# One block kernel: attention's transfers issued later, turned token groups split in alternation, half of the first norms on ScalarE, one store moved

## The chip, the cores and the metric

The kernel runs on one core of one Trainium2 chip. The metric is the device time of one execution in microseconds (us): the median of three runs, and one more execution under the hardware profiler.

## What is computed

The input is 2048 tokens of width 576. They are normalized, and the normalized tokens go two ways: through attention with 32 heads of width 18 and a sliding window of 256, and through a gated feed-forward block with a 2048 x 2048 matrix that mixes tokens. The two results are multiplied and added to the input.

```
xn = layernorm(x)
q, k, v = split(xn @ wqkv)                       # 32 heads of 18
o = softmax(mask(q k^T / sqrt(18), 0 <= i - j < 256)) v
s = o @ wo
z = gelu(xn @ w_in);  z1, z2 = halves of 2304
g = w_sp @ layernorm(z2) + b_sp                  # over tokens
out = x + s * silu((z1 * g) @ w_out)
```

## The kernel before, in words

All products run in float32 halves: an operand is split into a high part (rounded by ScalarE, `split`, L112) and a low part (the difference, by VectorE, L113), and three products of halves are summed. TensorE is the engine with most of the work. The other engines' instructions, and the queue of SyncE (SP), which issues every DMA, stand in an order that the Python code writes out by hand; each queue is worked off strictly in that order, so an instruction that waits holds up what stands behind it.

The stages, in order of time:

- **Tokens in, q and k (0 to 156 us).** Tokens come in four chunks of 512 (`load_x`). VectorE takes their means and variances (`stats_of`, `scales_of`), and a norm writes them to `xpair` (on VectorE for chunk 0, `norm_dve` L316; on ScalarE for the others, `norm_act` L323). TensorE turns them in groups (`turn_group`, L333): group one has planes 0 to 3, group two planes 4 to 7, each in one PSUM tile `tpt`, and group three plane 8, in a tile that one of the first two has to give back. The function that `turn_group` returns splits a group plane by plane: high by ScalarE, low by VectorE. The planes lie in `b0` to `b5`. Then the weights of q and k, fetched into three buffers `wraw` and split by ScalarE (`wqh`) and GpSimd (`wql`), are multiplied with the planes: first narrow products of 256 columns (`first_steps` L418, `narrow` L369), then wide ones of 512 (`qk_wide`, L203). Each result is split into `qkhl` and stored in `st_d` by four DMAs (`keep_chunk` L359, `keep` L352).
- **v, z2 (156 to 440 us).** The same planes times other weights.
- **Attention (440 to 950 us).** There are 16 units (4 heads by 1024 tokens). For a unit, rows q and k of its heads are loaded from `st_d` into slots `att` (L539): 16 DMAs at the start of each unit, called a burst below, of which the first 8 are for the second pair of heads of the next unit and the last 8 for the first pair of the one after. A burst stands behind four small DMAs `att<-mhl` (L619) that bring in row maxima. Scores for the maxima (`sp`, L589), scores for the exponentials (`tps`, L713, exponentials `pt` on ScalarE L717, masks on GpSimd L725 and L728) and the product with v (`ops`, L741) are put in order by a planner: it keeps a clock, gives each instruction a fixed cost, and takes a loaded pair as there 5500 ns after its last load is issued (`LOAD_NS`). Where nothing is ready it fills in products of z1 (L660), whose weights `z1raw` (L629) ScalarE splits (`z1wh`, L675) and whose results `z1o` are stored in `z_d` (L562 calls the store).
- **The end of a unit** (`finish`): denominators `den` are loaded from `ou` (L803), VectorE inverts them (L776), they are stored in `r_d` (L778) and fetched back spread over partitions by four DMAs `rp` (L783, 128 KB each), GpSimd multiplies (`divide`, L787, four pieces), and four DMAs store `o_d` (L792). The times of these steps after the end of the unit, in the planner's ns, are the constants `INVERT_AT`, `FETCH_AT` (after the store of `r_d`) and `DIVIDE_AT` (four divides, four stores).
- **Output of attention (950 to 1010 us)**, with `ohl` (L1123) split from `o_d`; **mixing over tokens (to about 1715 us)** and **last product with silu (to 1939 us)**.

Of the kernel before, what the change touches and what calls it, by code (L numbers as in the profile page):

```python
# [16 lines left out]
P = 128  # L17
# [27 lines left out]
MAX_NS = 5000  # L45
INVERT_AT = 7500
FETCH_AT = 3500
DIVIDE_AT = (18000, 19500, 21000, 22500, 23500, 24000, 24500, 25000)
WARM = 54
# [7 lines left out]
def f32(ap):  # L57
    return ap.bitcast(F32)
# [3 lines left out]
def kernel(  # L62
# [169 lines left out]
    with ExitStack() as early:  # L232
# [17 lines left out]
        with ExitStack() as ph:  # L250
# [75 lines left out]
            def turn_group(c, ks):  # L326

                t = tp.tile([P, 2, 512], F32, name="tpt")
                for n, k in enumerate(ks):
                    for i in range(2):  # L330
                        for h, r in enumerate(ROWS):
                            c0 = (2 * n + i) * 64
                            pe.transpose(t[:, h, c0:c0 + 64], xpair[c][i][r, k].rearrange("p a b -> p (a b)"),  # L333
                                         ident[r, r])

                def form():
                    for n, k in enumerate(ks):
                        src = t[:, :, n * P:(n + 1) * P].rearrange("p h (i d) -> p i h d", i=2)
                        cs = slice(c * 256, (c + 1) * 256)
                        hi, lo = (plane(m, cs).rearrange("p (i h d) -> p i h d", i=2, h=2) for m in (k, 9 + k))  # L340
                        split(hi, lo, src)

                return form

# [53 lines left out]
            for tiles in ((0, 1), (2, 3)):  # L398
                stats_of(0, tiles)
                scales_of(0, tiles)  # L400
            for i in range(4):
                done = norm_dve(0, i)
# [17 lines left out]

            forms[0]()
            forms[1]()
            first_steps(WL_LAST[0:8])
            turn_group(0, [8])()
            first_steps(WL_LAST[9:17])
            first_steps([24, 25])
# [22 lines left out]
            load_x(3)  # L449
            forms[0]()  # L450
            forms[1]()
            scales_of(2, range(4))
            banks = narrow(4, 0)
            turn_group(1, [8])()
            fetch(6, w_qk[6])
            keep_narrow(4, 0, banks)
            for j in range(5):
                banks = narrow(j, 1)
                if j < 2:
                    fetch(7 + j, w_qk[7 + j])  # L460
                if j == 3:
                    forms = [turn_group(2, range(0, 4)), turn_group(2, range(4, 8))]
                keep_narrow(j, 1, banks)
                done = None
                if j < 2:
                    norm_act(2, (2 * j, 2 * j + 1))
                if j == 0:
                    stats_of(3, range(4))
                if j == 1:
                    done = scales_of(3, range(4))  # L470
                if j == 3:
                    forms[0]()
                    forms[1]()
                if j == 4:
                    turn_group(2, [8])()
                    norm_act(3, range(4))
                if j < 4:
                    wq_high(5 + j)
                    low = wq_low(5 + j)
                    if done:  # L480
                        behind(low, done)
            for j in range(5, 9):
                if j < 8:
                    fetch_v(0, j - 5)
                for n in qk_wide(j, 0):
                    if j == 6 and n in (3, 9, 18):
                        turn_group(3, (range(0, 4), range(4, 8), [8])[(3, 9, 18).index(n)])()
                if j < 8:
                    split_v(wv, 0, j - 5)
            tokens.close()  # L490
# [18 lines left out]
        with ExitStack() as ph:  # L509
# [138 lines left out]
            def z1_rows(r):  # L648

                for f in range(FH // P):  # L650
# [6 lines left out]
                    for b in range(2):  # L657
                        ps = fillp.tile([P, 512], F32, name=("ma", "mb")[r])
                        for n, (w, x_) in enumerate(moving_x(wh, wl, slice(b * 512, (b + 1) * 512), r)):
# [3 lines left out]
                            if n == STEPS - 1:  # L663
                                zo = zw.tile([P, 512], F32, name="z1o", bufs=3)
                                act.activation(zo, ps, AF.Copy)  # L665
                                bank_free[r] = use("act", 480, 120) + 100
                                after(bank_free[r] - clock + 100,
                                      partial(sp.dma_start, z1_tokens[f * P:(f + 1) * P, b, :, r],
                                              zo.rearrange("p (a q) -> p a q", a=2)))
# [99 lines left out]
            def finish(u, ou):  # L769
# [5 lines left out]
                def invert():  # L775
                    dve.reciprocal(den, den)  # L776
# [207 lines left out]
            with ExitStack() as heads:  # L984
# [64 lines left out]
                while score_queue[0] or score_queue[1] or todo or filling:  # L1049
# [498 lines left out]
```

## Time and profile before

| what | value |
|---|---|
| median of the runs | 1942.09 us (1939.25 to 1943.32, three runs) |
| the profiled execution: its own time, its span | 1941.25 us, 1939.5 us |
| TensorE busy, share of the span | 1876.8 us, 97% |
| VectorE, ScalarE, GpSimd busy | 1038.2, 914.3, 397.6 us |
| granted TensorE clock, mean | 0.984 |
| DMA: moved, mean rate | 389.85 MB, 201 GB/s |

The span runs from the first to the last instruction. In the rows of the timeline, the columns are start in us, duration in us, engine, line, operation, output and inputs, shape, count, and in brackets the idle time of the engine before the row and what ended it. SPq rows are DMA issues. In rows of waits the columns are the total in us, the number of waits and the longest. A row of windows gives, after the stretch and its length, the busy time of TensorE, of its weight loads, of VectorE, ScalarE and GpSimd with the number of instructions, then the granted clock, the DMA share and GB/s.

### The profile page before, as it was taken

What the parts mean: (1) busy time and instruction counts of PE and PEld (TensorE: products, weight loads), DVE (VectorE), ACT (ScalarE), POOL (GpSimd) and SP (SyncE); (2) the same over time, 40 slices, a digit from 0 to 9 for tenths busy, and PEclk for the clock granted to TensorE, in tenths of its full rate; (3) what the DMA queues carried; (4) which work ended last, traced back from release to release, by engine and by line L of the source; (5) the groups of instructions that cost most, each with busy time, mean ns of one, the idle gap of its engine ahead of it and who ended that gap; (6) DMA issues with size and microseconds to landing.
All of it is one profiled execution on the core that took longest, in us unless ns stands there. A gap on an engine that the chain in (4) does not pass through costs nothing.

```text
span 1939.5 us, 38538 instructions
## 1 busy us (share of the span) xinstructions
PE 1876.8 (97%) x14552; PEld 1627.8 (84%) x14552; DVE 1038.2 (54%) x2275; ACT 914.3 (47%) x1758; POOL 397.6 (20%) x486
## 2 busy tenths in 40 slices
PE   8999999999999998999899999999999999999999
PEld 7899999997777776766698878888888888899998
DVE  5411333456567655654227787747786667563222
ACT  4523322324656654666548575555454534442111
POOL 3322333434455444545300000000000000000000
PEclk7999999999999998999899999999999999999999
DMA  7786688885656655564577777766676555875441
GB/s 228 181 222 181 215 280 277 285 279 150 166 162 177 184 147 151 151 177 113 181 248 261 234 243 237 248 221 217 199 251 234 184 176 180 272 231 155 143 141 58
DMA packets 234314, 389.85 MB, mean 201 GB/s; under 512 B 51984, under 2 KB 145680, under 8 KB 234000
## 3 DMA queue, kind: packets, MB, share of 16 engines
q1 hardware_dynamic: 234128, 387.39, 64.6%
q8 instruction: 114, 1.87, 0.4%
q14 instruction: 72, 0.59, 0.1%
HBM read 274.74 MB, written 111.78 MB: 199 GB/s over the span
## 4 chain that ended last, share of the span: by engine, by line
PE 78%; DMA 9%; DVE 5%; SPq 3%; issue 2%; ACT 2%; POOL 1%; POOLq 0%; DVEq 0%; ACTq 0%
PE acc L1378 31%; PE po L1471 12%; PE mb L203 10%; PE ma L660 5%; PE ma L203 4%; PE mb L660 4%; PE ops L741 4%; DMA att<-st_d 3%; PE tps L713 2%; PE sp L589 2%; PE wops L1137 2%; DMA z1raw<-in_w_z_dram 1%; SPq L352 1%; DMA den<-ou 1%; DMA st_d<-qkhl 1%
## 5 line engine op out<-in xcount | busy, mean ns | idle before, releaser
L1378 PE MATMUL acc<-spl,zh 128*128 128x512 f32 x1008 | 392.6, 390 | 1.9 <-DVE spl L113 1.7
L1378 PE MATMUL acc<-sph,zh 128*128 128x512 f32 x1008 | 392.2, 389 | 0.0
L1378 PE MATMUL acc<-sph,zl 128*128 128x512 f32 x1008 | 392.1, 389 | 0.0
L593 DVE CUSTOM_DVE_ANT_0 junk<-sp,band 128x384 bf16<-128x384 f32 (+1 forms) x512 | 275.8, 539 | 177.5 <-PE sp L589 78.3
L717 ACT ACTIVATE pt<-tps 128x384 f32<-128x384 f32 (+2 forms) x576 | 230.3, 439 | 151.3 <-PE tps L713 102.5
L660 PE MATMUL mb<-b,z1wh 64*128 64x512 f32 x648 | 228.2, 406 | 0.4 <-ACT z1o L665 0.3
L660 PE MATMUL ma<-b,z1wh 64*128 64x512 f32 x648 | 227.0, 406 | 0.5 <-ACT zt L935 0.4
L1378 PEld LDWEIGHTS acc<-spl,zh 128*128 128x128 f32 x1008 | 189.2, 188 | 42.9 <-DVE spl L113 3.5
L113 DVE TENSOR_TENSOR spl<-spr,sph 128x1024 fp32r<-128x1024 f32 x168 | 205.6, 1224 | 32.8 <-ACT sph L112 32.2
L1378 PEld LDWEIGHTS acc<-sph,zh 128*128 128x128 f32 x1008 | 189.2, 188 | 39.6
L1378 PEld LDWEIGHTS acc<-sph,zl 128*128 128x128 f32 x1008 | 189.2, 188 | 38.6
L112 ACT ACTIVATE zh<-b 128x384 fp32r<-128x384 f32 x168 | 87.4, 520 | 230.3 <-PE acc L1378 230.3
L713 PE MATMUL tps<-att 56*128 56x384 f32 (+1 forms) x576 | 180.3, 354 | 10.4 <-ACT pt L717 7.7
L589 PE MATMUL sp<-att 54*128 54x384 f32 (+1 forms) x512 | 162.8, 359 | 19.5 <-DMA att<-st_d 14.6
L112 ACT ACTIVATE sph<-spr 128x1024 fp32r<-128x1024 f32 x168 | 175.8, 1047 | 2.1 <-DMA spr<-in_w_sp_dram 1.3
L113 DVE TENSOR_TENSOR zl<-b,zh 128x384 fp32r<-128x384 f32 x168 | 93.4, 556 | 147.0 <-ACT zh L112 146.9
L1471 PE MATMUL po<-b,yh 128*128 128x288 f32 x840 | 147.2, 295 | 0.5 <-ACT gs L1458 0.5
L713 PEld LDWEIGHTS tps<-att 56*128 56x128 f32 x576 | 100.7, 189 | 41.9 <-ACT pt L717 16.6
L660 PE MATMUL ma<-b,z1wl 64*128 64x512 f32 x324 | 130.3, 402 | 0.0
L660 PE MATMUL mb<-b,z1wl 64*128 64x512 f32 x324 | 130.1, 402 | 0.0
L589 PEld LDWEIGHTS sp<-att 54*128 54x128 f32 x512 | 89.7, 189 | 45.1 <-issue 22.8
L660 PEld LDWEIGHTS ma<-b,z1wh 64*128 64x128 f32 x648 | 119.9, 190 | 6.6 <-issue 1.8
(232 smaller groups left out, 4228.5 us busy)
## 6 DMA issues: line engine op xcount, KB each, us to landing
spr<-sc_d SPq DMA_DIRECT2D x96, 512.0 KB
spr<-in_w_sp_dram SPq DMA_DIRECT2D x72, 512.0 KB
zr<-z_d SPq DMA_DIRECT2D x144, 192.0 KB
z_d<-zt SPq DMA_DIRECT2D x48, 384.0 KB
z_d<-z1o SPq DMA_DIRECT2D x72, 256.0 KB
z1t<-z_d SPq DMA_DIRECT2D x72, 256.0 KB
y_d<-z1t SPq DMA_DIRECT2D x72, 256.0 KB
a<-in_w_sp_dram SPq DMA_DIRECT2D x64, 256.0 KB
```

The source lines that it names most:

```text
L112: act.activation(hi, src, AF.Copy)
L113: dve.tensor_tensor(lo, src, f32(hi), ALU.subtract)
L203: pe.matmul(banks[h][:, :n], *both[h][i], start=i == 0, stop=i == STEPS - 1)
L589: pe.matmul(ps[:, :w], q_of(u, j)[0:54, i * P:(i + 1) * P], k_of(u, j)[0:54, k0:k0 + w], start=True, stop=True)
L593: dve.tensor_tensor_reduce(out=junk[:, :w], in0=ps[:, :w], in1=band[:, m0:m0 + w], scale=1.0, scalar=-3.0e38, op0=ALU.add, op1=ALU.max, ac ...
L660: pe.matmul(ps, w, x_, start=n == 0, stop=n == STEPS - 1)
L713: pe.matmul(ps[:, :m * P], k_of(u, j)[:, (kb - base) * P:(kb - base + 1) * P], q_of(u, j)[:, (a - lo) * P:(a - lo + m) * P], start=True, s ...
L717: act.activation(pt[:, j, d0:d0 + n * P], ps[:, (qa - a) * P:(qa - a + n) * P], AF.Exp, scale=scale)
L741: pe.matmul(o_ps[c][32 * j:32 * j + 32, (qa - 4 * c) * P:(hi - 4 * c + 1) * P], vgs[u][:, kb - k0, j * VW:j * VW + 32], pt[:, j, (qa - kb) ...
L1137: pe.matmul(po[:, i, :288], lt[:, cs], r[:, i * 288:(i + 1) * 288], start=n == 0, stop=n == len(pl) - 1)
L1378: pe.matmul(acc[j], z[:, ps], w[:, cs], start=s == i == 0 and n in OPENS, stop=s == 7 and i == 2, skip_group_check=True)
L1471: pe.matmul(po[i][:, a, :288], y if ahead else y[:, i * P:(i + 1) * P], w[a], start=f == 0 and m == 0, stop=f == NF - 1 and m == 2)
```

## The change

Five edits:

1. The function returned by `turn_group` is now a list of pieces, and `form(*groups)` splits two groups in alternation: the high halves of plane k of both groups on ScalarE, then both low halves on VectorE. The first products on chunk 0 take the planes in that order (0, 4, 1, 5, ...).
2. Of the four norms of chunk 0, those of tiles 0 and 1 go to ScalarE (`norm_act`).
3. The splits of the first half of v's weights (`split_v(wv, ...)`) come one product later, so behind the splits of chunk 3.
4. In attention the store of `z1o` comes 1200 instead of 100 ns after the planned copy; the load of `den` 1000 instead of 300; inversion, store of `r_d`, fetch of `rp`, the divides and the stores of `o_d` all later.
5. At the end of attention, what the planner has due within 3000 ns is issued ahead of the loads for the output product, the rest behind them.

```
-INVERT_AT = 7500
-FETCH_AT = 3500
-DIVIDE_AT = (18000, 19500, 21000, 22500, 23500, 24000, 24500, 25000)
+KEEP_NS = 1200
+INVERT_AT = 9000
+FETCH_AT = 7500
+DIVIDE_AT = (22500, 24000, 25500, 27000, 31000, 31500, 32000, 32500)
...
+            def form(*groups):
+                for pieces in zip(*groups):
+                    for hi, _, src in pieces:
+                        act.activation(hi, src, AF.Copy)
+                    for hi, lo, src in pieces:
+                        dve.tensor_tensor(lo, src, f32(hi), ALU.subtract)
...
                 scales_of(0, tiles)
-            for i in range(4):
+                if tiles[0] == 0:
+                    norm_act(0, tiles)
+            for i in (2, 3):
                 done = norm_dve(0, i)
...
-            forms[0]()
-            forms[1]()
-            first_steps(WL_LAST[0:8])
-            turn_group(0, [8])()
-            first_steps(WL_LAST[9:17])
+            form(*forms)
+            ready = (0, 4, 1, 5, 2, 6, 3, 7)
+            first_steps([3 * k for k in ready])
+            form(turn_group(0, [8]))
+            first_steps([3 * k + 1 for k in ready])
...
-                if j < 8:
-                    split_v(wv, 0, j - 5)
+                if j > 5:
+                    split_v(wv, 0, j - 6)
...
-                                after(bank_free[r] - clock + 100,
+                                after(bank_free[r] - clock + KEEP_NS,
...
-                    after(t, lambda: sp.dma_start(r_d[u].rearrange("h (a b) -> (h a) b", b=HS // 32), den))
+                    after(t + 1500, lambda: sp.dma_start(r_d[u].rearrange("h (a b) -> (h a) b", b=HS // 32), den))
...
-                    after(busy["act"] - clock + 300, lambda: sp.dma_start(den, ou[DH::32, :]))
+                    after(busy["act"] - clock + 1000, lambda: sp.dma_start(den, ou[DH::32, :]))
...
-                oraws += [wo_load(t) for t in range(1, 3)]
-                while waiting:
-                    clock += 100000
-                    tick()
+                for ns in (3000, 100000):
+                    waiting.sort(key=lambda w: w[0])
+                    while waiting and waiting[0][0] <= clock + ns:
+                        waiting.pop(0)[1]()
+                        waiting.sort(key=lambda w: w[0])
+                    if ns == 3000:
+                        oraws += [wo_load(t) for t in range(1, 3)]
```

**ScalarE, the first chunk, before.** `tpt_248` and `tpt_265` are the PSUM tiles of groups one and two, `tpt_336` that of group three; `st` are statistics.

```order
L116 ACTIVATE st1_205<-st2_204,eps_t_87 128x2 x2
L265 ACTIVATE wqh_242<-wraw_189 128x1152
L265 ACTIVATE wqh_245<-wraw_191 128x1152
L112 ACTIVATE b0_92<-tpt_248 128x256 x3
L112 ACTIVATE b1_93<-tpt_248 128x256
L112 ACTIVATE b1_93<-tpt_265 128x256 x2
L112 ACTIVATE b2_94<-tpt_265 128x256 x2
L112 ACTIVATE b2_94<-tpt_336 128x256
```

The same place in the changed kernel (lines past 333 have other numbers there).

```order
L117 ACTIVATE st1_205<-st2_204,eps_t_87 128x2
L324 ACTIVATE xpair_222<-xr_181,st3_206,st4_207 128x9x64
L324 ACTIVATE xpair_223<-xr_183,st3_206,st4_207 128x9x64
L117 ACTIVATE st1_205<-st2_204,eps_t_87 128x2
L266 ACTIVATE wqh_242<-wraw_189 128x1152
L266 ACTIVATE wqh_245<-wraw_191 128x1152
L349 ACTIVATE b0_92<-tpt_248 128x256
L349 ACTIVATE b1_93<-tpt_265 128x256
L349 ACTIVATE b0_92<-tpt_248 128x256
L349 ACTIVATE b1_93<-tpt_265 128x256
```

Two norms now stand between the two square roots, and the reads go to the two tiles in turn.

**SP, the second burst of attention, before** (the one at 512.38 us in the trace of before): the DMAs from the store of `r_d` to the burst's eighth load.

```order
L778 DMA r_d<-den 128x32
L783 DMA rp<-r_d 32x1024
L562 DMA z_d<-z1o 128x2x256
L783 DMA rp<-r_d 32x1024 x3
L562 DMA z_d<-z1o 128x2x256
L619 DMA att_6848<-mhl 2x8x128 x2
L619 DMA att_2227<-mhl 2x8x128 x2
L539 DMA att_2229<-st_d 36x1024
L539 DMA att_2229<-st_d 18x1024 x2
L539 DMA att_2229<-st_d 36x1024 x2
L539 DMA att_2229<-st_d 18x1024 x2
L539 DMA att_2229<-st_d 36x1024
```

The same place in the changed kernel, from the row maxima to the eighth load.

```order
L627 DMA att_6848<-mhl 2x8x128 x2
L627 DMA att_2227<-mhl 2x8x128 x2
L547 DMA att_2229<-st_d 36x1024
L791 DMA rp<-r_d 32x1024
L547 DMA att_2229<-st_d 18x1024
L791 DMA rp<-r_d 32x1024
L547 DMA att_2229<-st_d 18x1024
L791 DMA rp<-r_d 32x1024
L547 DMA att_2229<-st_d 36x1024
L791 DMA rp<-r_d 32x1024
L547 DMA att_2229<-st_d 36x1024
L547 DMA att_2229<-st_d 18x1024 x2
```

The four fetches of `rp`, which stood ahead of the maxima, now stand among the first loads. The same holds for the next five bursts, through the one at 648.32 us.

**SP, the burst at 716.54 us, before**, from the maxima to the third load.

```order
L619 DMA att_6846<-mhl 2x8x128 x2
L619 DMA att_6848<-mhl 2x8x128 x2
L783 DMA rp<-r_d 32x1024 x4
L562 DMA z_d<-z1o 128x2x256
L792 DMA o_d<-ou 18x1024
L539 DMA att_2228<-st_d 36x1024
L792 DMA o_d<-ou 18x1024
L539 DMA att_2228<-st_d 18x1280
L629 DMA z1raw<-in_w_z_dram 128x1152
L792 DMA o_d<-ou 18x1024
L562 DMA z_d<-z1o 128x2x256
L539 DMA att_2228<-st_d 18x1024
```

The same place in the changed kernel.

```order
L627 DMA att_6846<-mhl 2x8x128 x2
L627 DMA att_6848<-mhl 2x8x128 x2
L786 DMA r_d<-den 128x32
L570 DMA z_d<-z1o 128x2x256
L791 DMA rp<-r_d 32x1024 x4
L547 DMA att_2228<-st_d 36x1024
L637 DMA z1raw<-in_w_z_dram 128x1152
L547 DMA att_2228<-st_d 18x1280
L547 DMA att_2228<-st_d 18x1024
L547 DMA att_2228<-st_d 36x1280
L570 DMA z_d<-z1o 128x2x256
L547 DMA att_2228<-st_d 36x1024
```

The four stores of `o_d` are gone from among the loads (they now stand behind the burst before, with the same unit's divides ahead of them on GpSimd), and `z1raw` has moved up.

More of the change, by code (lines that the diff above doesn't have):

```diff
@@ L334, in turn_group @@
                                          ident[r, r])
[L336 to L343, printed above, removed]
+                pieces = []
+                for n, k in enumerate(ks):
+                    src = t[:, :, n * P:(n + 1) * P].rearrange("p h (i d) -> p i h d", i=2)
+                    cs = slice(c * 256, (c + 1) * 256)
+                    hi, lo = (plane(m, cs).rearrange("p (i h d) -> p i h d", i=2, h=2) for m in (k, 9 + k))
+                    pieces.append((hi, lo, src))
+                return pieces
+            def form(*groups):
[4 more added lines that the diff above has]
+                        dve.tensor_tensor(lo, src, f32(hi), ALU.subtract)
             st_v = st_d.rearrange("n r h (b a g p) -> n r h b a g p", b=2, a=2, g=2)
@@ L449 @@
             load_x(3)
-            forms[0]()
-            forms[1]()
+            form(*forms)
             scales_of(2, range(4))
             banks = narrow(4, 0)
-            turn_group(1, [8])()
+            form(turn_group(1, [8]))
             fetch(6, w_qk[6])
@@ L471 @@
                 if j == 3:
-                    forms[0]()
-                    forms[1]()
+                    form(*forms)
                 if j == 4:
-                    turn_group(2, [8])()
+                    form(turn_group(2, [8]))
                     norm_act(3, range(4))
@@ L486 @@
                     if j == 6 and n in (3, 9, 18):
-                        turn_group(3, (range(0, 4), range(4, 8), [8])[(3, 9, 18).index(n)])()
-                if j < 8:
-                    split_v(wv, 0, j - 5)
+                        form(turn_group(3, (range(0, 4), range(4, 8), [8])[(3, 9, 18).index(n)]))
+                if j > 5:
+                    split_v(wv, 0, j - 6)
             tokens.close()
```

## The prediction

> **What bounds the kernel now.** I read the table of windows first, for four stretches cut at the stages.
>
> ```profile
> 0.00:95.00 95.00, 81.66 (x952) 75.48 (x954) 48.55 (x150) 45.93 (x93) 30.20 (x22) 0.87 0.72 205
> 95.00:440.00 345.00, 343.13 (x3974) 338.30 (x3973) 122.75 (x245) 95.66 (x211) 121.02 (x109) 1.00 0.79 246
> 440.00:960.00 520.00, 479.68 (x4468) 362.10 (x4465) 292.09 (x1047) 307.28 (x745) 242.82 (x355) 0.96 0.58 161
> 960.00:1939.00 979.00, 972.37 (x5167) 851.89 (x5165) 574.80 (x834) 465.44 (x710) 3.53 (x2) 1.00 0.64 206
> ```
>
> The first busy time is TensorE's. It leaves 13.3 us idle up to 95 us, 40.3 us in attention (440 to 960), and 1.9 and 6.6 us elsewhere. TensorE is the bound, the change touches none of its work, and so it can win only from these idle times and from the clock they cost (the column 0.87 and 0.96). The waits of TensorE grouped by what released it follow.
>
> ```profile
> PE sp L589 <- DMA att<-st_d: 14.6, 8, 2.9
> PE tps L713 <- ACT pt L717: 7.7, 4, 4.1
> ```
>
> In attention what ends last is mostly a load `att`: 14.6 us in 8 waits, at most 2.9. One of them in the timeline, and the window of 4 us behind it:
>
> ```profile
> 491.88 0.38 PE L589 MATMUL sp<-att 54*128 54x256 f32 x2 [1.94 <-DMA att<-st_d]
> 492.00:496.00 4.00, 4.00 (x28) 3.92 (x30) 2.09 (x9) 1.78 (x4) 1.23 (x2) 0.64 0.82 196
> ```
>
> The granted clock is 0.64 in that window, so (1 - 0.64) x 4 = 1.4 us are lost beyond the wait of 1.94, in all some 3.4. I take 1.5 us for such a dip, and that not every wait has one is a source of error. The Trainium skill, "TensorE: Matmul & The Clock Gate", section "Why this matters for your kernels", says that only idle gaps of over about 3 us between bursts of matmuls bring the half clock back. The trace disagrees (1.94 us was enough); by that rule the dips behind the shorter gaps below would drop out on both sides, and the sum would come out about 1.4 us later.
>
> **The front (0 to 95 us).**
>
> ```profile
> 10.88 3.21 DVE L316 TENSOR_SCALAR xpair<-xr,st,st 128x576 f32<-128x576 f32 x4
> 15.19 0.38 ACT L112 ACTIVATE b<-tpt 128x256 fp32r<-128x256 f32 x1 [3.38 <-PE tpt L333]
> ...
> 20.77 0.38 ACT L112 ACTIVATE b<-tpt 128x256 fp32r<-128x256 f32 x1 [0.49 <-DVE b L113]
> 22.68 0.42 DVE L113 TENSOR_TENSOR b<-tpt,b 128x256 fp32r<-128x256 f32 x1 [1.07 <-ACT b L112]
> 29.02 0.38 PE L369 MATMUL ma<-b,wqh 64*128 64x256 f32 x1 [0.74 <-DVE qkhl L113]
> 30.25 3.15 ACT L323 ACTIVATE xpair<-xr,st,st 128x576 f32<-128x576 f32 x4
> ```
>
> Four norms on VectorE take 3.21 us, 0.80 each; on ScalarE 3.15, as long. Two of them go to an engine that stood idle (3.38 us before its first split), so the chain of VectorE is 2 x 0.80 = 1.6 us shorter. The high parts of planes 0 and 7 are 20.77 - 15.19 = 5.58 us apart, 0.80 per plane: each 0.38 on ScalarE waits for the 0.42 on VectorE before it, because both read the same PSUM tile. In alternation the pace is VectorE's 0.42, and 7 x (0.80 - 0.42) = 2.7, less about 0.5 for the turns of the second group, which are now needed sooner: 2.2 us. Together 3.8. TensorE waits at 29.02 for VectorE's `qkhl`, at the end of the same chain, so I take it in full; at the least the 0.74 of that wait.
>
> ```profile
> 41.98 0.34 PE L333 MATMUL tpt<-ident,xpair 64*128 64x64 f32 x4 [1.99 <-DVE b L113]
> ...
> 79.10 0.34 PE L333 MATMUL tpt<-ident,xpair 64*128 64x64 f32 x4 [3.61 <-DVE b L113]
> 80.00:84.00 4.00, 4.00 (x24) 3.59 (x22) 2.38 (x6) 2.72 (x6) 0.00 (x0) 0.57 0.36 82
> 90.60 17.75 SPq L352 DMA_DIRECT2D st_d<-qkhl  x24
> ```
>
> On chunk 1 the third group of turns waits 1.99 us for the splits of a tile; faster splits take away 1.5 of it (bounds 0.4, what one plane saves, and 4, the wait with a clock dip). On chunk 3 the same turn waits 3.61 us, since the splits stand on ScalarE behind `wvh`, whose weights come late by DMA; `split_v` one product later removes that: 3.6, plus (1 - 0.57) x 4 = 1.7 of clock, less 0.3 for the splits themselves: 5.0. The later `wvh` now stands in front of nothing that is due within a product. Front: 3.8 + 1.5 + 5.0 = 10.3. Behind it lies a stretch in which SP's queue is the limit: 24 stores in a row take 17.75 us, 0.74 each. When TensorE comes there sooner it can end up waiting for a `qkhl` that has not been stored. I give 1.3 back (all of it but 1: rival C): 9.0.
>
> **Attention, the losses.**
>
> ```profile
> 512.38 5.65 SPq L539 DMA_DIRECT2D att<-st_d  x12
> 520.74 0.62 PE L589 MATMUL sp<-att 54*128 54x256 f32 x3 [0.25 <-DMA att<-st_d]
> 560.28 1.72 SPq L783 DMA_DIRECT2D rp<-r_d  x4
> ...
> 669.54 2.72 SPq L783 DMA_DIRECT2D rp<-r_d  x4
> ```
>
> In the six bursts from 512.38 to 648.32 the four `rp` move from ahead of the maxima in among the first eight loads. The planner fixes TensorE's order by the issue of the last load and not by what SP has in between, and the first loaded pair is used the moment it lands (the wait of 0.25 at 520.74). Four `rp` hold SP for 1.72 us in one place and 2.72 in another. I take 1.8, nearest to the row that is undisturbed, in each of six bursts: 10.8; the bounds are 0 (if the planner's products of z1 cover it, rival B) and 2.72 x 6 = 16.3. Two of these new waits will cost a dip: 3.0. Loss 13.8.
>
> The Trainium skill, "DMA: Bandwidth & Descriptors", section "Queues, rings and completion order", adds that on each DMA engine descriptors are consumed in ring order, which speaks against the change: a load issued behind `rp` waits for its bytes as well, not for SP alone. No run here separates the two; it belongs to rival D.
>
> **Attention, the gains.**
>
> ```profile
> 558.47 0.35 DVE L776 RECIPROCAL den<-den 128x32 f32<-128x32 f32 x1 [3.48 <-DMA den<-ou]
> 559.29 0.44 PE L589 MATMUL sp<-att 54*128 54x384 f32 x1 [1.99 <-DVE mx L593]
> ...
> 720.39 5.81 SPq L539 DMA_DIRECT2D att<-st_d  x7
> 727.98 0.41 PE L589 MATMUL sp<-att 54*128 54x384 f32 x1 [1.98 <-DMA att<-st_d]
> 730.09 0.69 PE L589 MATMUL sp<-att 54*128 54x384 f32 x2 [1.71 <-DMA att<-st_d]
> ...
> 754.83 0.37 SPq L629 DMA_DIRECT2D z1raw<-in_w_z_dram  x1
> 761.19 0.74 PE L713 MATMUL tps<-att 56*128 56x256 f32 x2 [4.13 <-ACT pt L717]
> 862.92 0.41 PE L589 MATMUL sp<-att 54*128 54x384 f32 x1 [2.91 <-DMA att<-st_d]
> 894.27 0.44 PE L589 MATMUL sp<-att 54*128 54x384 f32 x2 [2.68 <-DMA att<-st_d]
> ```
>
> At 558.47 the inversion waits 3.48 us for its `den`; the maxima behind it on VectorE come late, and TensorE waits 1.99 at 559.29. Inverted 1.5 us later, with the load only 0.7 later, the wait falls: 2.0 + 1.4 of clock = 3.4. In the burst at 716.54 the stores of `o_d`, which wait for GpSimd, stand among the loads (12 loads took 5.65 us at 512.38, 7 take 5.81 here). They leave, and two waits with a dip each go: 1.98 + 1.71 + 3.0 = 6.7. At 754.83 `z1raw` is fetched late, `z1wh` on ScalarE waits for it with the exponentials behind it, and TensorE waits 4.13 for `pt`; with `z1raw` further ahead I take half of the group's 7.7, 3.9, and one dip, 1.5: 5.4. From the waits of 2.91 and 2.68, again in bursts with `o_d`, 3.5 of 5.6 (`rp` comes into those bursts). Gains 19.0, net 19.0 - 13.8 = 5.2.
>
> **The end of attention.**
>
> ```profile
> 948.49 0.47 SPq L562 DMA_DIRECT2D z_d<-z1o  x1
> 951.99 1.27 ACT L1123 ACTIVATE ohl<-spare 128x1280 fp32r<-128x1280 f32 x1 [5.34 <-DMA z_d<-z1o]
> 953.31 6.87 PE L1137 MATMUL wops<-att,ohl 128*128 128x288 f32 x35 [7.43 <-ACT ohl L1123]
> ```
>
> The split `ohl` waits 5.34 us for a store of `z_d` that stands behind the stores of `o_d`; TensorE waits 7.43 with it. The store goes ahead of the loads, and about half of that, 3.3, could go (the queue in front of it is not gone).
>
> ```profile
> 976.22 0.65 ACT L1170 ACTIVATE so<-wops 128x576 f32<-128x576 f32 x1 [8.18 <-DMA s_d<-so]
> ```
>
> But the chain den, r_d, rp, divide, `o_d`, `s_d` of the last unit, which ScalarE waits 8.18 us for at 976.22, starts only 1 to 2 us sooner and takes the place of the wait: 2.0, between 0.6 and 5.
>
> **The sum.** 9.0 + 5.2 + 2.0 = 16.2 us off the profiled execution's own 1941.25: 1925.0. The median of the runs is 0.84 higher, so 1926.
>
> **Rivals.** A is the sum above. *B: the fetches of `rp` cost nothing*, because products of z1 stand ready to fill in, or because the wait of 0.25 shows loads that SP does not set. Then 13.8 come back: 1926 - 13.8 = 1912. For it speaks that `rp` was ahead of the burst before, on the same queue, without a wait of more than 0.25 at 520.74. *C: the front's gain is lost in the stretch of 24 stores*, whose 17.75 us hold SP's queue: 9 becomes 1, 1934. Against it stands that TensorE is 343.13 of 345.00 us busy there, with waits of 1.9 in all, so the stores do keep up today. *E: half of the second half's gains* (6.7, 5.4, 3.5 and 3.4, 19.0) come, since `r_d` and `rp` come into bursts that `o_d` leaves: 9.5 less, 1935.5. *D, slower: `rp` among the loads pays in all thirteen bursts that now have it*, 13 x 1.8 = 23.4, and six waits dip, 9.0: 32.4 lost, and in the later bursts the gains shrink to 3.4 + 5.4 + 9.0 (front) + 2.0 (end) = 19.8. 1942.1 - 19.8 + 32.4 = 1954.7. It decides from 19.8 / 2.5 = 8 bursts that pay 1.8 and half a dip. For it speaks the trace at 727.98 and 730.09: DMAs between loads did cost TensorE there. Against it: those waited for GpSimd, and the four `rp` do not, since `r_d` is stored well ahead of them.
>
> **How the numbers follow.** A 0.50, B 0.20, C 0.11, E 0.09, D 0.10. A's own range is 1918 to 1933: the loss of `rp` between 10.8 - 6 and 16.3, the end between 0.6 and 5, chunk 1 between 0.4 and 4. The range for 8 in 10 reaches from beyond B's 1912 (-3, the end at its upper bound) to beyond E's 1935.5 (+2.5): 1909 to 1938. A difference under 0.2%, 3.9 us, is what a measurement of this kernel can't tell from none. Faster by more (under 1938.2): A, B and most of C and E, 0.85. Within it: 0.06, from the upper ends of C and E and the point at which D turns. Slower: 0.09, D.
>
> **What would show it.** The first product behind chunk 0's (now at 29.02) should start near 25.2; the turn at 79.10 should have no wait of 3.6, and the clock no dip behind it; from 95 to 156 us no new waits for `qkhl` should stand (they would be C). In the bursts two to seven of attention TensorE should wait about 2 us each time for `att` (none: B; and if also from 716 on: D). The bursts from 716 on should lose their waits of 1.7 to 2.9, and the wait for `pt` should fall below 4. Ahead of `wops` TensorE should idle some 4 to 5 us instead of 7.43. The prediction is wrong if TensorE's idle time in attention stays at 40 us or more, or if the front is not some 9 us shorter at the first product of v.

## The result, and the profile after

The changed kernel takes 1928.95 us (median of 4 runs, 1925.75 to 1930.69) beside 1942.7 for the kernel before; the ratio is 0.9927, with a 95% interval of 0.9905 to 0.9950. By the ratio that is 14.2 us, where 16.2 were forecast (1926). The profiled execution has a span of 1927.4 us, 12.1 less than before.

The windows of the changed kernel for three of the same four stretches (columns as before: TensorE's busy time first, the granted clock third from the end; from 95 to 440 us it is again 1.00):

```profile
0.00:95.00 95.00, 87.98 (x1064) 83.64 (x1066) 48.98 (x152) 50.03 (x99) 31.91 (x22) 0.96 0.81 228
440.00:960.00 520.00, 475.49 (x4454) 359.19 (x4451) 286.56 (x1012) 306.62 (x744) 242.78 (x353) 0.97 0.58 158
960.00:1939.00 979.00, 961.11 (x5084) 840.64 (x5082) 572.11 (x832) 462.18 (x704) 0.00 (x0) 1.00 0.63 205
```

TensorE's idle time up to 95 us has fallen from 13.3 to 7.0, and the clock there has risen from 0.87 to 0.96. In attention it idles 44.5 us of the same stretch, not less than the 40.3 before. (The last stretch holds 11.6 us after the end.) These windows are fixed in time, and the changed kernel reaches each place sooner; cut from the first scores to the first output product, before and then the changed kernel, they are:

```profile
411.19:953.31 542.12, 500.12 (x4725) 381.07 (x4723) 312.43 (x1125) 310.97 (x756) 254.44 (x364) 0.97 0.59 167
398.17:942.41 544.24, 497.51 (x4725) 378.30 (x4722) 313.68 (x1125) 310.08 (x756) 254.69 (x364) 0.97 0.60 167
```

So TensorE idles 42.0 us there before and 46.7 in the changed kernel, and the gain is in the front. A sharper measure is how much sooner TensorE starts the same instruction, counted by line, in the two traces. Rows are places in the program, with their time in the kernel before:

| place in the kernel before | changed kernel is ahead by |
|---|---|
| first product of chunk 1, 29.0 us | 4.5 |
| first wide product, 63.4 us | 7.7 |
| products of v, 116.8 us | 13.1 |
| first scores, 411.2 us | 13.0 |
| scores at 489.7 us | 13.6 |
| scores at 684.8 us | 0.6 |
| scores at 785.5 us | 8.2 |
| output product, 953.3 us | 10.9 |
| mixing over tokens, 1016.5 us | 11.2 |
| last product, 1935.1 us | 12.1 |

13.0 us are won in the front. Between 490 and 685 us, 13.0 are lost again; 10.3 come back by 953. Attention as a whole gives 10.9 - 13.0 = -2.1, its end 0.3.

**The front** in the changed kernel:

```profile
13.40 3.51 ACT L349 ACTIVATE b<-tpt 128x256 fp32r<-128x256 f32 x8 [1.55 <-PE tpt L334]
13.81 3.55 DVE L351 TENSOR_TENSOR b<-tpt,b 128x256 fp32r<-128x256 f32 x8 [1.25 <-ACT b L349]
24.48 0.58 PE L377 MATMUL ma<-b,wqh 64*128 64x256 f32 x1 [2.11 <-DVE qkhl L114]
38.22 0.34 PE L334 MATMUL tpt<-ident,xpair 64*128 64x64 f32 x4 [1.21 <-DVE b L351]
67.62 0.30 PE L334 MATMUL tpt<-ident,xpair 64*128 64x64 f32 x4
```

Eight high halves take 3.51 us, 0.44 each, where a plane took 0.80: the two engines now work on two tiles at a time. The clock of the first chunk moved too, from 12 to 24 us before and then in the changed kernel:

```profile
12.00:24.00 12.00, 9.91 (x86) 8.02 (x88) 6.68 (x16) 4.40 (x10) 5.46 (x3) 0.50 0.52 172
12.00:24.00 12.00, 9.88 (x144) 9.24 (x144) 8.83 (x29) 5.97 (x16) 7.93 (x3) 0.86 0.71 247
```

In windows of half a microsecond the clock before is 0.50 from 12.0 to 25.5 us, in the changed kernel from 14.5 to 17.5 only. The turn on chunk 1 waits 1.21 instead of 1.99. The turn on chunk 3, now at 67.62, has no idle time in brackets: its 3.61 are gone. Windows of 4 us behind the last two:

```profile
40.00:44.00 4.00, 4.00 (x75) 4.00 (x73) 2.34 (x8) 2.24 (x5) 0.00 (x0) 1.00 0.96 343
67.00:71.00 4.00, 4.00 (x40) 3.65 (x38) 2.62 (x7) 2.47 (x8) 0.00 (x0) 1.00 0.80 166
```

The clock is 1.00 in both. Before, it was this in two windows of 4 us at the place on chunk 1:

```profile
42.00:46.00 4.00, 3.59 (x30) 2.83 (x32) 2.48 (x12) 2.16 (x7) 0.00 (x0) 0.57 0.98 284
46.00:50.00 4.00, 4.00 (x46) 4.00 (x44) 1.17 (x4) 0.66 (x3) 0.00 (x0) 0.58 0.92 295
```

So on chunk 1 the dip was worth (0.43 + 0.42) x 4 = 3.4 us, more than the wait.

**Attention.** Two groups of TensorE's waits in the changed kernel, then SP's queue and TensorE at the burst at 582.61, and two of the later waits:

```profile
PE sp L597 <- DMA att<-st_d: 16.4, 10, 4.0
PE tps L721 <- ACT pt L725: 6.2, 4, 3.9
```

```profile
582.61 0.72 SPq L547 DMA_DIRECT2D att<-st_d  x2
583.37 0.31 SPq L791 DMA_DIRECT2D rp<-r_d  x1
583.72 0.33 SPq L547 DMA_DIRECT2D att<-st_d  x1
584.10 0.77 SPq L791 DMA_DIRECT2D rp<-r_d  x2
584.91 0.39 SPq L547 DMA_DIRECT2D att<-st_d  x1
585.34 0.34 SPq L791 DMA_DIRECT2D rp<-r_d  x1
585.94 0.38 SPq L570 DMA_DIRECT2D z_d<-z1o  x1
586.41 6.42 SPq L547 DMA_DIRECT2D att<-st_d  x12
...
592.66 0.52 PE L597 MATMUL sp<-att 54*128 54x256 f32 x3 [1.49 <-DMA att<-st_d]
...
622.51 0.55 PE L597 MATMUL sp<-att 54*128 54x256 f32 x1 [2.38 <-DMA att<-st_d]
...
655.73 0.59 PE L597 MATMUL sp<-att 54*128 54x384 f32 x2 [3.99 <-DMA att<-st_d]
```

Four `rp` and a store stand between the first and the eighth load, and the scores wait for them: 1.49 here, 2.38 and 3.99 in the next two bursts. The waits for loads have grown from 14.6 to 16.4 us although of those of 2.91 and 2.68 late in attention the one has fallen to 0.8 and the other has gone. At the end the wait ahead of `wops` is 7.4, as before; only what ends it is another DMA:

```profile
937.29 1.54 SPq L800 DMA_DIRECT2D o_d<-ou  x4
...
941.09 1.27 ACT L1134 ACTIVATE ohl<-spare 128x1280 fp32r<-128x1280 f32 x1 [5.42 <-DMA o_d<-ou]
...
942.41 7.87 PE L1148 MATMUL wops<-att,ohl 128*128 128x288 f32 x44 [7.40 <-ACT ohl L1134]
```

### The profile page after: what moved, and what is told of

The parts are those of the page before. It is cut to its first block, busy times and chain, and to the rows that moved or that the text cites. A ratio compares the mean times of both kernels' runs of the same rounds, so it can differ in the third digit from the quotient of the medians.

```text
span 1927.4 us, 38537 instructions
## 1 busy us (share of the span) xinstructions
PE 1867.1 (97%) x14552; PEld 1619.2 (84%) x14552; DVE 1037.9 (54%) x2273; ACT 916.3 (48%) x1760; POOL 397.8 (21%) x486
## 4 chain that ended last, share of the span: by engine, by line
PE 76%; DMA 11%; DVE 5%; SPq 4%; issue 2%; ACT 2%; POOL 0%; POOLq 0%; DVEq 0%; ACTq 0%
PE acc L1389 32%; PE po L1482 12%; PE mb L204 9%; PE ma L204 5%; PE ma L668 4%; DMA att<-st_d 3%; PE ops L749 3%; PE mb L668 3%; PE tps L721 2%; PE sp L597 2%; PE wops L1148 2%; SPq L360 2%; DMA z1raw<-in_w_z_dram 2%; DMA st_d<-qkhl 1%; DMA rp<-r_d 1%
## 5 line engine op out<-in xcount | busy, mean ns | idle before, releaser
L114 DVE TENSOR_TENSOR spl<-spr,sph 128x1024 fp32r<-128x1024 f32 x168 | 205.4, 1223 | 32.6 <-ACT sph L113 32.1
L597 PE MATMUL sp<-att 54*128 54x384 f32 (+1 forms) x512 | 161.0, 356 | 18.1 <-DMA att<-st_d 16.4
L1482 PEld LDWEIGHTS po<-b,yh 128*128 128x128 f32 x840 | 124.2, 188 | 0.7 <-ACT gs L1469 0.7
```

What stands on the lines that cost most here:

```text
L114: dve.tensor_tensor(lo, src, f32(hi), ALU.subtract)
L597: pe.matmul(ps[:, :w], q_of(u, j)[0:54, i * P:(i + 1) * P], k_of(u, j)[0:54, k0:k0 + w], start=True, stop=True)
L1482: pe.matmul(po[i][:, a, :288], y if ahead else y[:, i * P:(i + 1) * P], w[a], start=f == 0 and m == 0, stop=f == NF - 1 and m == 2)
```

## The experiments

The theory: the front's gain passes to the end whole, the later stores of `o_d` win in attention about what was forecast, and `rp` among the first loads costs more than forecast and takes it back. The rivals: the loss comes from something else that was moved later (z1 stores, inversion), or from bursts that come at another moment. Each kernel was compared with the kernel before on the same chip. The results, with what each trace has won against before at four places (by the measure above):

| kernel | ratio to before | 95% interval | scores 411.2 | scores 489.7 | scores 684.8 | output product |
|---|---|---|---|---|---|---|
| changed kernel | 0.9927 | 0.9905 to 0.9950 | 13.0 | 13.6 | 0.6 | 10.9 |
| e1, front alone | 0.9932 | 0.9911 to 0.9954 | 13.5 | 13.2 | 14.7 | 15.5 |
| e2, attention's constants alone | 0.9987 | 0.9973 to 1.0001 | 0.0 | -1.4 | -17.8 | -5.3 |
| e3, `rp` ahead of the maxima | 0.9815 | 0.9791 to 0.9839 | 13.9 | 14.7 | 17.4 | 33.5 |
| e4, `rp` of an eighth of the bytes | 0.9847 | 0.9826 to 0.9867 | 11.7 | 11.7 | 5.3 | 21.2 |
| e5, `rp` among the last eight loads | 1.0052 | 1.0035 to 1.0068 | 14.6 | 15.3 | -22.0 | -8.8 |
| e6, e3 with early z1 stores | 0.9860 | 0.9836 to 0.9884 | 12.4 | 11.4 | 3.2 | 19.3 |
| e7, e3 with early last divides | 0.9829 | 0.9805 to 0.9853 | 13.1 | 12.9 | 13.1 | 31.6 |
| e8, `rp` in eight pieces | 0.9966 | 0.9951 to 0.9982 | 12.9 | 13.8 | -8.1 | -0.8 |
| e9, front without alternation | 0.9951 | 0.9934 to 0.9968 | 6.2 | 5.4 | 3.0 | 0.7 |
| e10, `rp` among first loads for seven units | 0.9881 | 0.9861 to 0.9901 | 14.6 | 15.3 | 1.9 | 20.7 |
| e11, e3 with z1 stores later still | 0.9824 | 0.9804 to 0.9844 | 14.2 | 12.3 | 9.5 | 28.2 |

A step of 0.001 is 1.9 us. The columns of places come from one execution each: kernels with the same front differ by up to 3 us at 411.2, and e3 and e7, whose programs are the same up to the end of attention, by 4.3 at 684.8.

**e1, the front alone.** The constants and the flush of before in the changed kernel:

```
-KEEP_NS = 1200
-INVERT_AT = 9000
-FETCH_AT = 7500
-DIVIDE_AT = (22500, 24000, 25500, 27000, 31000, 31500, 32000, 32500)
+KEEP_NS = 100
+INVERT_AT = 7500
+FETCH_AT = 3500
+DIVIDE_AT = (18000, 19500, 21000, 22500, 23500, 24000, 24500, 25000)
```

> Only the three edits of the front (alternating splits, two norms on ScalarE, split_v one product later); attention and its end as before. Theory 1 (the front's gain passes to the end whole, and edits 4 and 5 give about nothing together): the first scores come 13.0 us sooner, as in the changed kernel, and the kernel ends 13 us sooner, 1929.7 us against 1942.7. Rival (the front's gain is given back in attention, because its waits only end later or sooner with other dips): 13.0 at the first scores, but 5 us or less at the end, 1937 or more.

Ratio 0.9932: 13.2 us, with 13.5 at the first scores. The gain passes to the end whole, and the front alone is as fast as the whole change (0.9927). Edits 4 and 5 together add nothing that can be measured.

**e2, attention's constants alone**: the reverse of the diff above (but for the flush) in the kernel before.

> Only the constants of attention (edit 4); the front and the end of attention as before. Theory 1 (gains of the later o_d stores and losses of rp among the loads cancel): within 3 us of before, 1940 to 1946, and in the trace a loss of about 14 us against before over the bursts from 569 to 672 us, given back partly behind them. Rival (the prediction's net gain of 5.2): 1937.5.

Ratio 0.9987, 2.5 us, and an interval that reaches 1.0001. The trace loses 16.4 us between 490 and 685 and has 12.5 of them back at the output product: gains and losses cancel here too. The forecast of 5.2 (0.9973) stands at the edge of the interval.

**e3, `rp` ahead of the maxima.**

```
-FETCH_AT = 7500
+FETCH_AT = 3500
```

> The changed kernel with FETCH_AT at 3500 as before: the four rp of every unit stand ahead of the row maxima again, not among the first loads; nothing else moves. Theory 1 (rp among the first loads is what costs 14 us between 577 and 685 us of before): the waits of scores for att in those bursts fall from 1.5 to 4.0 to under 0.5, and the kernel takes about 1917 us, 12 less than the changed one's 1929. Rival (the loss is from the z1 stores and the inversion, which were moved later as well, or from bursts that come at another moment): within 3 us of 1929.

Ratio 0.9815, 21.8 us less than the changed kernel. No instruction of TensorE, VectorE, ScalarE or GpSimd changes its place; one number moves `rp` on SP's queue. The theory's cause holds, and the rivals fall, since the z1 stores and the inversion stay as late as they were; but the gain is nearly twice the 12 us expected, and one wait for `att` of 1.89 stays (at 611.01). Waits of TensorE inside attention, in e3:

```profile
PE sp L597 <- DMA att<-st_d: 5.5, 5, 1.9
PE tps L721 <- ACT pt L725: 4.4, 5, 3.4
```

The waits for loads fall from 16.4 to 5.5, 10.9 us. From the first scores to the first output product, e3 shows:

```profile
397.31:919.83 522.52, 490.45 (x4725) 372.80 (x4723) 313.95 (x1125) 309.51 (x756) 254.42 (x364) 0.99 0.62 174
```

Beside the changed kernel's row above, TensorE idles 32.1 us instead of 46.7, and its busy time for the same work falls by 7.1, with a clock of 0.99 instead of 0.97. So in these two executions some two thirds of the 21.7 us that this stretch is shorter are waits and one third is clock. And at the burst that answers to the one at 582.61, `rp` is away:

```profile
574.11 1.44 SPq L547 DMA_DIRECT2D att<-st_d  x4
575.65 0.38 SPq L570 DMA_DIRECT2D z_d<-z1o  x1
576.13 6.64 SPq L547 DMA_DIRECT2D att<-st_d  x12
```

**e4 and e8, bytes or issues.** The same four transfers at the same places, in e4 with 128 of 1024 columns (the divides use those eight times, so the output is another), in e8 as eight transfers of half the size.

```
-sp.dma_start(rp[32 * i:32 * i + 32, :], r_d[u][i:i + 1, :].to_broadcast([32, HS]))
+sp.dma_start(rp[32 * i:32 * i + 32, 0:P], r_d[u][i:i + 1, 0:P].to_broadcast([32, P]))
```

```
-sp.dma_start(rp[32 * i:32 * i + 32, :], r_d[u][i:i + 1, :].to_broadcast([32, HS]))
+[sp.dma_start(rp[32 * i:32 * i + 32, k:k + HS // 2], r_d[u][i:i + 1, k:k + HS // 2].to_broadcast([32, HS // 2]))
+ for k in (0, HS // 2)]
```

> The changed kernel with the same four rp transfers at the same places, each of 32 x 128 instead of 32 x 1024 (16 KB instead of 128 KB); the divides use those 128 columns eight times, so the softmax denominators are wrong beyond the first 128 rows. Theory A (rp costs by the time that SP takes to issue it, about 0.35 us each): no change, 1929 us, waits of 1.5 to 4.0 in the bursts as they are. Theory B (rp costs by its bytes, which the loads behind it wait for): the waits go as they do with rp ahead of the burst, about 1917 to 1919.

> The changed kernel with each rp split into two of 32 x 512 at the same place: the same bytes, twice the issues. e4 (an eighth of the bytes, the same issues, 1916) took back 12.5 of the 19.7 us between the changed kernel and e3, so that the issues should be worth about 7. Theory A+B (both cost, bytes about two thirds): 7 us slower than the changed kernel, 1936. Theory B (only bytes cost; what e4 did not take back are the remaining bytes and other causes): 1929, within 3.

e4 takes back 0.0080, 15.5 us, and stays 0.0032 (6.2 us) over e3. e8 is 0.0039 (7.6 us) slower than the changed kernel. The waits for loads inside attention, e4 and then e8:

```profile
PE sp L597 <- DMA att<-st_d: 11.0, 9, 2.1
```

```profile
PE sp L597 <- DMA att<-st_d: 24.9, 11, 3.8
```

With 5.5 in e3 and 16.4 in the changed kernel these stand in the order of the times. Neither theory holds alone: of about 22 us, some two thirds go with the bytes, a third with the issues (e8 doubles the pieces as well as the issues, and the runs do not tell these apart). That a load behind `rp` waits for its bytes agrees with the rule of the Trainium skill, "DMA: Bandwidth & Descriptors", section "Queues, rings and completion order", that descriptors are consumed in ring order.

**e5, `rp` among the last eight loads** of the burst for units 0 to 6, on top of e3; so that no divide comes ahead of its `rp`, the first divides of these units come 2.5 us later.

```
-after(t + FETCH_AT + 400 * i, partial(sums, i))
+after(t + (11500 if u < 7 else FETCH_AT) + 400 * i, partial(sums, i))
-after(ns, partial(part, u))
+after(ns + (2500 if u < 7 and ns < 28000 else 0), partial(part, u))
```

> As e3_rp_ahead (rp ahead of the maxima, 1909 us), but for units 0 to 6 the four rp stand among the last eight loads of the burst, with the first divides 2.5 us later. Those loads are used 10 us or more after their issue. Theory 1 (only the first eight loads have no slack): within 4 us of 1909, no waits over 1 us for att in those bursts beyond those of e3. Rival (rp costs wherever it shares the queue with loads, or the later divides make GpSimd's masks late): 1920 or more.

Slower than the kernel before: 1.0052. Two rows of TensorE's waits, two of GpSimd's queue and one of TensorE tell why:

```profile
PE ops L749 <- POOL pt L736: 34.2, 9, 6.5
...
PE sp L597 <- DMA att<-st_d: 5.5, 5, 1.4
```

```profile
POOL ou L795 <- DMA rp<-r_d: 14.4, 2, 8.7
...
610.32 0.72 POOL L795 TENSOR_TENSOR ou<-ou,rp 128x256 f32<-128x256 f32 x1 [8.57 <-DMA den<-ou]
...
612.27 1.51 PE L749 MATMUL ops<-pt,vg 128*32 128x384 f32 x8 [5.17 <-POOL pt L736]
```

The waits for loads, 5.5 us in all as in e3, agree with the first half of the theory (loads that are used 10 us later suffer nothing), but do not prove it: TensorE is held up elsewhere here, which may give the loads more time. The divide now comes to its turn on GpSimd before `rp` has landed; the masks `pt` stand behind it, and TensorE waits 34.2 us for them. (The divide at 610.32 reads `ou` and `rp`, not `den`: its last `rp` are issued from 603.77 to 605.67, and the load of `den` that the profile names is issued just behind, at 606.92.) It is the rival's second clause. Of the three places tried for `rp`, only the one ahead of the maxima costs nothing new.

**e6 and e11, the z1 stores**, on top of e3: `KEEP_NS = 100` as before, and `KEEP_NS = 2400`.

> As e3_rp_ahead, with the stores of z1 100 ns after the copy again (KEEP_NS as before). Theory 1 (the gain of attention comes from o_d, z1raw and the inversion, not from the z1 stores): 1909, within 4 us. Rival (a z1 store that waits for its copy holds SP's queue among the loads, and the 1200 ns take that away): 1915 to 1925, with waits for att of 0.5 to 2 us in several bursts.

> As e3_rp_ahead, with the stores of z1 2400 ns after the planned copy instead of 1200. Theory 1 (SP's wait for the copy, 15.0 us in e3 and 25.6 in e6, is what the constant buys): the wait for z1o falls further, and the kernel takes 1903 to 1907. Rival (1200 is enough, or the stores now land among the first loads and cost there as rp does): 1909 to 1914.

e6 is 0.0045 slower than e3, 8.7 us, with intervals that just touch; e11 is 0.0009 slower, nothing that can be told from none. The rival of the first holds, and 1200 is enough: in e11 SP's wait for the copy does fall on, from 15.0 us to 9.1, and nothing is won by it. A burst of e6, and what the scores then wait:

```profile
585.78 0.38 SPq L570 DMA_DIRECT2D z_d<-z1o  x1
586.21 8.77 SPq L547 DMA_DIRECT2D att<-st_d  x14
...
594.80 0.62 PE L597 MATMUL sp<-att 54*128 54x256 f32 x3 [2.02 <-DMA att<-st_d]
```

A store of 256 KB stands behind the second load, as `rp` did. That it costs in the same way is not shown apart from this wait.

**e7, earlier last divides**, on top of e3:

```
-for ns in DIVIDE_AT:
+for ns in DIVIDE_AT if u < NU - 2 else (18000, 19500, 21000, 22500, 23500, 24000, 24500, 25000):
```

> As e3_rp_ahead, with the divides and o_d stores of the last unit but one at the times of before (18 to 25 us instead of 22.5 to 32.5 after the unit). Theory 1 (at the end of attention ohl waits for these late o_d, which took the place of the z_d store that edit 5 moved): TensorE's wait ahead of wops falls from 7.5 to 4 or less, and the kernel takes 1904 to 1906. Rival (the chain of the last unit's den, r_d, rp, o_d bounds the end anyway): the wait falls, but the waits for s_d behind it grow by as much, 1909.

The two waits at the end of attention in e7,

```profile
921.73 24.58 PE L1148 MATMUL wops<-att,ohl 128*128 128x288 f32 x168 [5.11 <-ACT ohl L1134]
...
946.23 0.65 ACT L1181 ACTIVATE so<-wops 128x576 f32<-128x576 f32 x1 [8.59 <-DMA s_d<-so]
```

and the same in e3:

```profile
919.83 55.35 PE L1148 MATMUL wops<-att,ohl 128*128 128x288 f32 x396 [7.47 <-ACT ohl L1134]
...
941.81 0.65 ACT L1181 ACTIVATE so<-wops 128x576 f32<-128x576 f32 x1 [6.90 <-DMA s_d<-so]
```

The wait ahead of `wops` falls from 7.47 to 5.11, and the one for `s_d` behind it grows from 6.90 to 8.59. The ratio, 0.9829, is that of e3 within the intervals. So far as two traces can show it the rival holds: the chain of the last unit bounds the end.

**e9, the front without alternation**, on top of e1:

```
-for pieces in zip(*groups):
-    for hi, _, src in pieces:
-        act.activation(hi, src, AF.Copy)
-    for hi, lo, src in pieces:
-        dve.tensor_tensor(lo, src, f32(hi), ALU.subtract)
+for pieces in groups:
+    for hi, lo, src in pieces:
+        split(hi, lo, src)
...
-ready = (0, 4, 1, 5, 2, 6, 3, 7)
+ready = range(8)
```

> As e1_front (all edits of the front, attention as before, 13.5 us sooner at the first scores), but the groups are split one after the other as before; the two norms on ScalarE and split_v one product later stay. Theory 1 (alternation is worth 2.2 on chunk 0, and on chunk 1 the wait of 1.99 with its clock dip, 4.5 in all): the first scores come about 7 us sooner than before instead of 13.5, and the kernel takes about 1938 us on the scale on which before takes 1944. Rival (the earlier end of chunk 0, from the norms, is what lets chunk 1 come in time): within 2 us of e1_front, 1932.

```profile
41.23 0.34 PE L334 MATMUL tpt<-ident,xpair 64*128 64x64 f32 x4 [2.01 <-DVE b L114]
```

The wait on chunk 1 is back (2.01), and the first scores are only 6.2 us ahead. The ratio is 0.9951, 3.7 us from e1; the intervals overlap, so it is the trace that decides for theory 1. At 33.4 us of before, e9 is 0.8 ahead and e1 3.2, so alternation is worth 2.4 on chunk 0 and 4.6 on chunk 1, the norms 0.8, and the rest on chunk 3, 5.4, is `split_v`. What held the norms' gain down stands at the end of chunk 0, ahead of the first product of chunk 1:

```profile
27.80 0.42 DVE L114 TENSOR_TENSOR qkhl<-ma,qkhl 128x256 fp32r<-128x256 f32 x1 [0.85 <-ACT qkhl L113]
```

VectorE comes to this split 1.5 us sooner than in the kernel before (its step ahead of it starts at 26.77 instead of 28.29), as the norms should make it, but then waits 0.85 for ScalarE's high half, where it did not wait before. That half needs TensorE's last products of chunk 0, and starts only 0.7 sooner (27.38 instead of 28.12). The clock in e9 is 0.50 from 12.0 to 25.5 us, as before: without alternation TensorE itself, at half clock, holds up the end of the chunk.

**e10, `rp` among the first loads for units 0 to 6 only**, on top of e3:

```
-after(t + FETCH_AT + 400 * i, partial(sums, i))
+after(t + (7500 if u < 7 else FETCH_AT) + 400 * i, partial(sums, i))
```

> As e3_rp_ahead, but units 0 to 6 fetch rp among the first eight loads as the changed kernel does (FETCH_AT 7500 for them, 3500 for the later ones). Theory 1 (the loss is 16 us in these seven bursts and 6 in the later ones, as the stages of the two traces have it): about 1924, 5 less than the changed kernel. Rival of the prediction (only these bursts pay): 1929, the whole loss. Rival D's mechanism (all thirteen pay alike): 1919 or less.

Ratio 0.9881: seven bursts cost 0.0066, 12.8 us, and the later ones the other 0.0046, 8.9. The traces say about the same: from the scores at 489.7 to the output product e3 wins 18.8, e10 5.4, and the changed kernel loses 2.7, so 13.4 and 8.1. So the rival in which only these bursts pay falls: the six later units pay too, 1.5 each on average, beside 1.8 in the seven. (In the one at 699.2 of the changed kernel `rp` stands behind the maxima in e3 as well, so that not every one of the six can have paid.) By the ratio e10 takes 1920 us, nearer to 1919, where all pay alike, than to the 1924 of theory 1; but the interval reaches from 1916 to 1923, and the trace up to 685 has e10 16 behind e3, as theory 1 has it. These two are not told apart.

## Why the prediction was right or wrong

The total came out within 3 us, but by luck: it is made of errors that cancel. By the prediction's own signs its account of attention was wrong. It was to be wrong if TensorE's idle time there stayed at 40 us or more; that is 44.5 in the window it named, and 46.7 against 42.0 over the same work. The wait ahead of `wops` was to fall to 4 or 5 us and is 7.40, and of the waits in the bursts from 716 on, 1.72 and 0.8 stay. The signs for the front came true: its first product at 24.48 (25.2 forecast), no wait at the turn on chunk 3.

- **What bounds the kernel**: right. TensorE has the same work; all that moved is its idle time and the clock.
- **Front, 9.0 forecast, 13.0 in the trace** (13.5 in e1). Chunk 0: 3.8 forecast, 3.0 measured. The norms brought 0.8 for 1.6: the prediction followed VectorE's chain alone, and in e9 that chain ends 1.5 sooner but waits for TensorE, which is at half clock. Alternation brought 2.4 for 2.2, and that agreement is luck, for the pace of the splits is not all of it: the first product of chunk 1 comes 3.8 us sooner in e1 than in e9, since the half clock lasts 3.4 us instead of 13.7 and TensorE no longer ends last, and a new dip takes the rest back. Why the half clock is shorter with alternation, no run shows. At the first product of chunk 1 4.5 were won, of which a dip behind the new wait of 2.11 took 1.5. Chunk 3: 5.0 forecast, 5.4 measured. Chunk 1 is the mis-sized term: 1.5 forecast, 4.6 measured. I had the wait of 1.99 in the row and took only the wait; the clock dip behind it, 3.4 us in two windows, stood in the trace and I left it to the upper bound of 4. The 1.3 given back for the 24 stores did not come, and rival C falls; between 80 and 150 us the list of TensorE's waits has one row:

```profile
PE mb L204 <- DVE qkhl L114: 0.2, 1, 0.2
```

- **Attention's gains, 19.0 forecast**: e3, where `rp` costs nothing new, gains 33.5 - 13.9 = 19.6 between the first scores and the output product. Behind 685 us e3 wins 16.1, and the terms there were 6.7 + 5.4 + 3.5 = 15.6. That sum agrees better than its terms. The two waits at 727.98 and 730.09 gave 5.9 for 6.7. The wait for `pt` at 761.19, with its dip the 5.4, is still there in e3, and gave 1.2:

```profile
732.79 0.55 PE L721 MATMUL tps<-att 56*128 56x256 f32 x2 [3.39 <-ACT pt L725]
```

Instead 3.9 came from another wait for `pt`, of 2.46 at 696.51, and 6.1 where 3.5 were forecast (from 870 to 900 of before). And the z1 stores, which I priced at nothing, are worth 8.7 by e6, nearly all ahead of 685 in the traces. Without them the later inversion and `rp`, forecast at +3.4, do not win there: e6 loses 8.2 between 490 and 685, e3 wins 2.7.
- **Attention's losses, 13.8 forecast, 21.8 measured** (e3 against the changed kernel). This is the step that failed, and it failed on the count: I let six bursts pay, and `rp` stands close ahead of or among first loads in thirteen; by e10 the six last of these alone cost 8.9. The price per burst was somewhat too high: 21.8 / 13 = 1.7 with its clock, where 13.8 / 6 = 2.3 were forecast. That is rival D's count at two thirds of D's price (32.4 / 13 = 2.5); without the z1 stores' 8.7 the edits in attention would have made the kernel slower than the front alone.
- **The reason for that price was half right.** I took SP's time of 1.8; the bytes stood in rival D. By e4 and e8 about two thirds go with the bytes.
- **The end, 2.0 forecast, 0.3 measured.** `ohl` waits for the stores of `o_d`, whose divides the same change had made later, and where that wait is shortened (e7) the chain of the last unit takes it, as the prediction said it would.
- **Rival B** (`rp` costs nothing, 1912) was wrong as to the cause, but e3 shows that a kernel at its price existed: 1909.

The fastest version here is e3, the whole change but `FETCH_AT`, ratio 0.9815 to before; e7 and e11 are not told apart from it. What stays open is why the half clock of the first chunk is so much shorter with alternation, what the thirteen bursts cost one by one, and how the 21.8 divide into clock and wait in other executions than the two shown.

## What to carry to other kernels

When loads are used the moment they land, everything that is issued between the trigger and the last of them is on the critical path, with its bytes and its issue; count every place where the new order puts something there, not the ones that look worst. A transfer that nobody needs soon goes ahead of the trigger, or, which no run here tried in full, behind the last load if its consumer, and what stands behind that consumer on its engine, moves as far. A wait of TensorE is priced with the windows behind it: the clock may cost more than the wait. And a chain that ends just ahead of another wins only as far as the other, so both are followed before a gain is taken in full.

## What the runs showed of the hardware

The same wait can cost the clock or not. The first product of chunk 1 waits 2.11 us in the changed kernel (at 24.48) and in e3:

```profile
24.24 0.38 PE L377 MATMUL ma<-b,wqh 64*128 64x256 f32 x1 [2.11 <-DVE qkhl L114]
```

The 4 us from 24 on, the changed kernel and then e3:

```profile
24.00:28.00 4.00, 3.52 (x31) 3.47 (x33) 1.43 (x5) 3.98 (x5) 2.66 (x1) 0.57 0.51 122
```

```profile
24.00:28.00 4.00, 3.76 (x61) 3.61 (x63) 1.18 (x4) 3.89 (x6) 2.68 (x1) 1.00 0.55 136
```

0.57 in one, 1.00 in the other: 1.7 us for the same gap. In the kernel before, the wait of 2.91 at 862.92 has no dip behind it, and that of 1.94 at 491.88 has 0.64:

```profile
863.00:867.00 4.00, 4.00 (x45) 3.22 (x47) 2.72 (x10) 2.71 (x6) 0.74 (x2) 1.00 0.79 178
```

In the thirteen traces, from 30 to 960 us, all 39 gaps of over 3 us are followed by a half clock within 4 us, and so are 51 of the 77 between about 1.5 and 3 us. The Trainium skill, "TensorE: Matmul & The Clock Gate", section "Why this matters for your kernels", puts the bound at about 3 us; here shorter gaps often cost it, in e1 one of 1.48 us at 478.28 (0.57 over the 4 us from 478).

A half clock also comes in steps of time. Of its 124 stretches in these traces, 60 last 3.4 us, 33 last 6.8, 15 last 10.2 and 3 last 13.7. Where TensorE has work throughout, each step of 3.4 us costs half of it, 1.7. The three of 13.7 us are the first chunk of the kernel before, of e2 and of e9; in the ten kernels with alternation that stretch lasts 3.4.
